# Attention fused with an RWKV channel mix on one core: a new written-out order of pieces, with four zeros matmuls fewer

## The chip, the cores and the metric

The kernel runs on 1 core of one Trainium2 chip (8 cores, of which one is used). The metric is the device time of one execution in microseconds. TensorE is called PE here, VectorE DVE, ScalarE ACT, GpSimd POOL and SyncE SP.

## The reference

For 8 batches, 8 heads, 576 rows and a head width of 64, a linear attention is followed by a channel mix of width 512 with a hidden width of 1024:

```python
kv = np.einsum('bhsd,bhse->bhde', k, v)
u = np.einsum('bhsd,bhde->bhse', q, kv)
rms = np.sqrt(np.mean(u * u, axis=-1, keepdims=True) + 1e-06)
x = (u / rms * g_norm)             # heads side by side: (B, S, 512)
x_prev = x shifted by one row
xk = mu_k * x + (1.0 - mu_k) * x_prev
xr = mu_r * x + (1.0 - mu_r) * x_prev
kk = np.maximum(xk @ w_k, 0.0)
out = sigmoid(xr @ w_r) * (kk * kk @ w_v)
```

All inputs and the output are fp32; the kernel multiplies in bf16.

## The kernel before

The work is cut into some 660 named pieces. Each piece issues a handful of instructions on one engine, and a string `ORDER` names them one after another. `Plan.emit` walks through that string and calls each piece; nothing is rearranged afterwards, so an engine runs its pieces in the order of the string, and an engine that waits holds up everything behind it in its own queue. A suffix `@A` or `@D` puts a piece on ACT or DVE where both can do it. `z:512` issues one matmul of zeros with 512 columns (line 437, into a PSUM buffer that the first stage-two product will overwrite).

A batch `b` goes through attention, with `z` (0 or 1) the half of the heads. For batch 0 the halves are separate pieces; for later batches one piece `.01` does both.

- `ldh.k`, `ldh.v`: SP loads the first half of k and v of batch 0 as fp32 (line 236, into memory that later holds `xk`); `cst.k0`, `cst.k1`, `cst.v0`, `cst.v1` cast them to bf16 (lines 128 on ACT, 130 on DVE).
- `ld.*`: POOL issues all other loads of q, k, v (lines 221, 226) and of the weights (line 252), which cast on the way. POOL's own queue waits for buffers and for a free slot of eight.
- `kv`: k transposed times v on PE (line 265). `kc` copies it, `ks` permutes it on PE (line 271), `kd` copies it again.
- `tq`: DVE transposes q (line 349). `u`: q times kv on PE (line 282).
- `uc`: u times g_norm into SBUF (lines 134, 136). `sq`: the squares, on ACT (line 370).
- `ss`, `rs`: sums of squares on PE (lines 395, 379) and reciprocal root on ACT (line 288). From batch 2 on `rs` is made once per head and `sp` spreads it over partitions with four DMAs of SP each (line 417).
- `mul` (line 392), `d` (line 300), `mk`/`mr` (lines 134, 136), `xk`/`xr` (line 313): the normed x, its difference to the row before, and the two blends.

Rows are then taken in nine groups `g` of 512: `k` (xk times w_k, lines 469 for g = 0, 493), `relu` (ACT, line 452), `ksq` (DVE, lines 480, 503), `r` (xr times w_r, line 515), `sig` (ACT, line 525), `v` (times w_v, line 535), `out` (the product, DVE, lines 548, 562), `st` (SP stores 128 rows, line 443). `tr9`, `cols` and `small` bring mu_k, mu_r and g_norm into columns: four small loads on SP, one fp32 matmul (line 211) and two DVE copies (lines 200, 201).

PSUM has four buffers `ps`, given out in turn. Two engines that read the same PSUM buffer wait for one another in the order of the string.

## Time and profile before

| | us |
|---|---|
| median of 3 timed runs | 201.87 (201.4 to 201.99) |
| the profiled execution, own time | 203.93 |
| its span from first to last instruction | 202.2 |
| PE busy | 190.9 |
| DVE busy | 134.3 |
| ACT busy | 125.0 |
| first matmul of zeros starts | 1.19 |
| last packet of `ldh.v` / `ldh.k` | 4.75 / 9.43 |
| first `kv` matmul starts | 9.97 |
| second `kv` starts | 15.14 |
| end of the last matmul | 198.2 |

The page gives busy time by engine; PE's is a model, as matmuls overlap, so the spacing of their starts tells more: 0.216 us between two matmuls of 512 columns at the full granted clock, and 0.427 us before 5.2 us. In the stretches (windows) each engine has its busy time and, in brackets, its number of instructions; then come the granted clock, the DMA share and GB/s. In the chain of waits each row is start, length, engine and line. In the timeline a row is start, length, engine, line, operation, what it writes and reads, how many, and in brackets how long the engine was idle before it and who ended that.

### The profile page before, as it was taken

The numbers are of one execution on the slowest core, as the hardware profiler recorded it, in microseconds if no ns is written. First come the engines' busy times: TensorE is split into PE (matmuls) and PEld (weight loads), VectorE is DVE, ScalarE is ACT, GpSimd is POOL, SyncE is SP. The second block draws the span as 40 slices with busy tenths as digits, with TensorE's granted clock in tenths as the row PEclk, the third lists the DMA queues.
The fourth block names the chain that finished last, engine by engine and source line by source line (L and its number), as shares of the span: only waits on it lengthen the run. The fifth ranks groups of instructions, "written<-read, shape, count | busy, mean of one in ns | idle before, by whom it ended". The sixth has DMA issues, their size and how long they took to land.

```text
span 202.2 us, 4282 instructions
## 1 busy us (share of the span) xinstructions
PE 190.9 (94%) x1769; PEld 93.8 (46%) x1769; DVE 134.3 (66%) x238; ACT 125.0 (62%) x163; POOL 23.3 (12%) x41
## 2 busy tenths in 40 slices
PE   7499897999999899999999999999999999999992
...
PEclk9999999999999999999999999999999999999999
...
GB/s 208 213 209 207 211 203 205 216 203 212 208 234 241 273 245 264 211 217 93 259 9 58 165 83 143 174 35 3 24 197 105 0 128 134 0 0 0 156 159 156
DMA packets 21015, 30.63 MB, mean 151 GB/s; under 512 B 1916, under 2 KB 14468, under 8 KB 20996
## 3 DMA queue, kind: packets, MB, share of 16 engines
...
q10 hardware_dynamic: 144, 0.13, 0.2%
...
## 4 chain that ended last, share of the span: by engine, by line
PE 76%; DMA 8%; DVE 7%; ACT 6%; SPq 1%; issue 1%; DVEq 0%
PE ps L535 28%; PE ps L493 26%; PE ps L515 14%; DMA xk<-in_k_dram 4%; DMA rs<-rsc 4%; ACT relu L452 2%; PE ps L282 2%; PE ps L265 2%; PE ps L437 1%; DVE xk L313 1%; DVE md L136 1%; DVE d L300 1%; ACT md L134 1%; DVE xT L392 1%; DVE uT L136 1%; ACT rs L288 1%
## 5 line engine op out<-in xcount | busy, mean ns | idle before, releaser
L535 PE MATMUL ps<-w_v,sqk 128*128 128x512 bf16 (+1 forms) x296 | 66.3, 373 | 0.9 <-ACT sq L370 0.9
L493 PE MATMUL ps<-xk,w_k 128*128 128x512 bf16 (+1 forms) x288 | 58.9, 356 | 1.0 <-DVE xk L313 1.0
L452 ACT ACTIVATE relu<-ps 128x1024 bf16<-128x1024 f32 x36 | 35.8, 1024 | 29.9 <-PE ps L493 28.9
L535 PEld LDWEIGHTS <-sqk 128*128 128x128 bf16 x296 | 28.3, 98 | 33.8 <-issue 2.7
L493 PEld LDWEIGHTS <-w_k 128*128 128x128 bf16 x288 | 27.3, 98 | 28.0 <-issue 1.9
L515 PE MATMUL ps<-w_r,xr 128*128 128x512 bf16 x144 | 34.4, 379 | 0.0
L548 DVE TENSOR_TENSOR out<-ps,sig 128x1024 f32<-128x1024 f32 x16 | 19.5, 1223 | 21.4 <-PE ps L535 9.4
L503 DVE TENSOR_TENSOR sqk<-relu 128x1024 bf16<-128x1024 bf16 x32 | 21.3, 686 | 12.4 <-ACT relu L452 12.4
L525 ACT ACTIVATE sig<-ps 128x1024 bf16<-128x1024 f32 x18 | 18.2, 1022 | 13.4 <-PE ps L515 13.2
L370 ACT ACTIVATE sq<-ps 128x576 bf16<-128x576 f32 x32 | 19.9, 653 | 4.8 <-PE ps L282 3.0
L515 PEld LDWEIGHTS <-xr 128*128 128x128 bf16 x144 | 13.8, 98 | 15.7 <-issue 0.2
L392 DVE TENSOR_TENSOR xT<-uT,rs 128x1152 bf16<-128x1152 bf16 (+1 forms) x18 | 12.3, 685 | 7.6 <-ACT rs L288 4.3
L136 DVE TENSOR_SCALAR md<-d,cols 128x576 bf16<-128x576 bf16 (+1 forms) x52 | 15.7, 352 | 0.4
L144 ACT ACT_TABLE_LOAD x12 | 15.4, 1283 | 0.9 <-PEq L588 0.7
L134 ACT ACTIVATE uT<-ps,cols 128x576 bf16<-128x576 f32 x19 | 13.6, 744 | 1.2 <-PE ps L282 1.1
L136 DVE TENSOR_SCALAR uT<-ps,cols 128x576 bf16<-128x576 f32 x13 | 10.5, 815 | 5.2 <-ACT sq L370 3.3
L134 ACT ACTIVATE md<-d,cols 128x576 bf16<-128x576 bf16 (+1 forms) x20 | 12.7, 699 | 1.6 <-DVE d L300 1.6
L437 PE MATMUL ps<-zero 128*128 128x512 bf16 x43 | 12.4, 435 | 1.2 <-DVE zero L164 1.2
L313 DVE TENSOR_TENSOR xk<-md,xT 128x1152 bf16<-128x1152 bf16 (+1 forms) x18 | 12.3, 688 | 1.8 <-ACT md L134 1.4
L313 DVE TENSOR_TENSOR xr<-md,xT 128x1152 bf16<-128x1152 bf16 (+1 forms) x18 | 12.0, 686 | 2.1 <-ACT md L134 2.0
L349 DVE STREAM_TRANSPOSE qT<-q 128x576 f32<-128x576 f32 (+1 forms) x18 | 13.2, 761 | 0.1
L300 DVE TENSOR_TENSOR d<-xT 128x1152 bf16<-128x1152 bf16 (+1 forms) x18 | 12.4, 692 | 0.4
...
## 6 DMA issues: line engine op xcount, KB each, us to landing
...
```

The lines of the kernel that those rows point to most:

```text
L134: nc.scalar.mul(out=dst, in_=src, mul=col)
L136: nc.vector.tensor_scalar(out=dst, in0=src, scalar1=col, scalar2=None, op0=ALU.mult)
L144: nc.scalar.preload_act_table_set(name)
L313: nc.vector.tensor_tensor(out=dst[:, 2 * z:2 * z + 2, r0:r0 + w], in0=md.t[:, :, cs], in1=xT[:, :, cur], op=ALU.add)
L370: sq_ = add("sq" + name, "A", lambda _, ps=ps, sq=sq, cs=cs, w=w: nc.scalar.activation(out=get(sq)[:, :, cs], in_=ps.t[:, :, 0:w], func=AF ...
L452: nc.scalar.activation(out=get(rt), in_=ps.t, func=AF.Relu)
L493: nc.tensor.matmul(get(ps)[:, fc % 2, a0:a1], w_k_sb[:, cc, 128 * fc:128 * fc + 128], xk[:, cc, x0:x0 + a1 - a0], start=(cc == 0), stop=(c ...
L503: nc.vector.tensor_mul(out=get(sqk)[:, 2 * f2:2 * f2 + 2, :], in0=rt.t, in1=rt.t)
L515: nc.tensor.matmul(get(ps)[:, ci % 2, :], xr[:, cc, n0:n0 + 128], w_r_sb[:, cc, :], start=(cc == 0), stop=(cc == NHP - 1))
L525: nc.scalar.activation(out=get(sg), in_=ps.t, func=AF.Sigmoid)
L535: nc.tensor.matmul(get(ps)[:, bank, cs], sqk.t[:, fc, 128 * ci:128 * ci + 128], w_v_sb[:, fc, cs], start=(fc == 0), stop=(fc == NFC - 1))
L548: dv = add(f"out{g}.{c2}", "D", lambda _, ps=ps, sg=sg, ot=ot: nc.vector.tensor_mul(out=get(ot), in0=ps.t, in1=sg.t), deps=ms + [sg_done], ...
```

## The change

`ORDER` is replaced by another one; no other line changes. The new string comes from a new search of the order and of the engines of all pieces, which was given later landings of the first loads, and in which the number of zeros matmuls is the least that a nominal and a late course ask for. It has 39 zeros matmuls instead of 43. All other pieces are the same. The beginning of the string, up to the two first weight products, as it was and as it is (the 16 zeros ahead of `kv0.0` and the loads ahead of them are the same):

```diff
- cst.v1@D cst.v0@A cst.k0@D cst.k1@D (z:512 x16) kv0.0 kc0.0@A z:512 z:512 ks0.0 tq0.0.0 tq0.0.1 tq0.1.0 small
-   z:512 z:512 tr9 cols kd0.0@A u0.0.1 uc0.01@A sq0.01 tq0.1.1 z:512 u0.0.0 sq0.00 (z:512 x7) kv0.1
-   ld.v3.01 ld.k3.01 ld.q3.01 uc0.00@D kc0.1@A ss0.01 ss0.00 rs0.01 ks0.1 mul0.01 kd0.1@A rs0.00 mul0.00
+ cst.v1@D cst.v0@A cst.k0@D cst.k1@A (z:512 x16) kv0.0 kc0.0@A z:512 z:512 ks0.0 tq0.0.0 tq0.0.1 tq0.1.0 small
+   tr9 cols kd0.0@A u0.0.1 uc0.01@A sq0.01 u0.0.0 uc0.00@D sq0.00 (z:512 x6) kv0.1
+   ld.k3.01 ld.v3.01 kc0.1@A ss0.01 tq0.1.1 ld.q3.01 ss0.00 rs0.01 mul0.01 ks0.1 kd0.1@A rs0.00 mul0.00
  (z:512 x3) u0.1.1 uc0.11@D sq0.11 u0.1.0 sq0.10 (z:512 x11) ss0.10 uc0.10@A d0.00 mk0.00@D xk0.00 k0.000
- k0.010 d0.01 mr0.01@D mk0.01@D xk0.01 ss0.11 rs0.10 mul0.10 d0.10 mr0.10@A k0.110
+ d0.01 mr0.01@D mk0.01@D xk0.01 ss0.11 rs0.10 mul0.10 d0.10 mr0.10@A k0.010 k0.110
```

Behind that, pieces change places all through the string, mostly by one to five positions. Those that change an engine or a queue's order, or that the prediction speaks of:

```diff
- relu0.11 u1.01.0 uc1.10@A ksq0.10 sq1.10 uc1.00@D u1.01.1
+ relu0.11 u1.01.0 uc1.00@D uc1.10@A ksq0.10 sq1.10 u1.01.1
- mul1.1 ss1.1 rs1.1 r0.0 r0.1 rs1.0 xr0.01 xr0.11 r0.2 mul1.0 d1.0 r0.3 d1.1
+ ss1.1 mul1.1 d1.1 rs1.1 r0.0 r0.1 rs1.0 xr0.01 xr0.11 r0.2 mul1.0 d1.0 r0.3
- kc2.01@A out0.1 k1.4 ... sp2.0 ... kv3.01 ld.k5.01 ld.q4.01 ld.v6.01 ld.v5.01 st0.1 st0.3 ksq1.1 st0.0
+ kc2.01@A out0.1 st0.3 k1.4 ... sp2.0 ... kv3.01 ld.k5.01 ld.q4.01 ld.v6.01 ld.v5.01 ld.q5.01 st0.1 ksq1.1 ... st0.0
- kv4.01 ld.k7.01 ld.q6.01 ld.v7.01 ld.q5.01 d2.1 uc3.00@A ss3 v1.2.1 ... k2.0 kd4.01@D ... k2.4 k2.1
+ ss3 d2.1 uc3.00@A kv4.01 ld.k7.01 ld.q6.01 ld.v7.01 v1.2.1 ... k2.0 k2.1 kd4.01@A ... k2.4
- kc6.01@D sp4.0 xr3.0 st2.2
+ kc6.01@A xr3.0 st2.2 ksq3.0 sp4.0
- uc6.10@D u6.01.1 xr4.0 uc6.00@A
+ uc6.10@D xr4.0 u6.01.1 uc6.00@D
- relu5.2 mr5.1@A xr5.1
+ mr5.1@D relu5.2 xr5.1
- mk6.0@D sq7.00 uc7.00@A r5.2 r5.3 ss7 mr6.1@D xk6.0 out5.0 rs7 k6.0 sp7.0 k6.1 xr6.1 st5.0
+ mk6.0@A sq7.00 uc7.00@A r5.2 r5.3 ss7 mr6.1@D xr6.1 xk6.0 out5.0 st5.0 rs7 sp7.0 k6.0 k6.1
```

More of the change, by code (lines that the diff above doesn't have):

```diff
@@ L15 @@
 ORDER = """
-ldh.v ldh.k ld.q0.0 ld.q0.1 ld.v0.1 ld.k0.1 ld.v1.0 seta zz setb setp ident perm ld.wk0 ld.k1.1 ld.wk1 ld.v1.1 ld.k1.0 ld.q1.01 ld.wv0 ld.wv1 ld.wr ld.k2.01 ld.v2.01 ld.q2.01 table cst.v1@D cst.v0@A cst.k0@D cst.k1@D z:512 z:512 z:512 z:512 z:512 z:512 z:512 z:512 z:512 z:512 z:512 z:512 z:512 z:512 z:512 z:512 kv0.0 kc0.0@A z:512 z:512 ks0.0 tq0.0.0 tq0.0.1 tq0.1.0 small z:512 z:512 tr9 cols kd0.0@A u0.0.1 uc0.01@A sq0.01 tq0.1.1 z:512 u0.0.0 sq0.00 z:512 z:512 z:512 z:512 z:512 z:512 z:512 kv0.1 ld.v3.01 ld.k3.01 ld.q3.01 uc0.00@D kc0.1@A ss0.01 ss0.00 rs0.01 ks0.1 mul0.01 kd0.1@A rs0.00 mul0.00 z:512 z:512 z:512 u0.1.1 uc0.11@D sq0.11 u0.1.0 sq0.10 z:512 z:512 z:512 z:512 z:512 z:512 z:512 z:512 z:512 z:512 z:512 ss0.10 uc0.10@A d0.00 mk0.00@D xk0.00 k0.000 k0.010 d0.01 mr0.01@D mk0.01@D xk0.01 ss0.11 rs0.10 mul0.10 d0.10 mr0.10@A k0.110 mk0.10@D xk0.10 k0.001 k0.011 rs0.11 mul0.11 relu0.00 d0.11 mk0.11@A xk0.11 ksq0.00 kv1.01 ld.k4.01 ld.v4.01 kc1.01@D mr0.00@D mr0.11@A relu0.01 k0.100 k0.101 relu0.10 tq1.01.1 tq1.01.0 ks1.01 kd1.01@A ksq0.01 k0.111 relu0.11 u1.01.0 uc1.10@A ksq0.10 sq1.10 uc1.00@D u1.01.1 sq1.11 ksq0.11 uc1.11@A sq1.00 v0.0.0 v0.1.0 xr0.00 xr0.10 ss1.2 sq1.01 rs1.2 ss1.3 rs1.3 v0.0.1 uc1.01@D ss1.0 v0.1.1 mul1.1 ss1.1 rs1.1 r0.0 r0.1 rs1.0 xr0.01 xr0.11 r0.2 mul1.0 d1.0 r0.3 d1.1 sig0.0 mk1.0@D xk1.0 sig0.1 out0.0 v0.2.0 v0.3.0 v0.3.1 v0.2.1 mk1.1@A xk1.1 mr1.0@A kv2.01 ld.k6.01 kc2.01@A out0.1 k1.4 ks2.01 kd2.01@A tq2.01.0 tq2.01.1 k1.5 relu1.2 u2.01.0 sq2.10 uc2.00@D sq2.00 uc2.10@D k1.2 k1.3 u2.01.1 sq2.11 uc2.01@D uc2.11@D k1.6 k1.7 mr1.1@D xr1.1 sq2.01 ss2 rs2 sp2.1 relu1.1 xr1.0 sp2.0 k1.0 k1.1 relu1.0 kv3.01 ld.k5.01 ld.q4.01 ld.v6.01 ld.v5.01 st0.1 st0.3 ksq1.1 st0.0 r1.0 r1.1 tq3.01.1 ksq1.0 r1.2 kc3.01@D relu1.3 ksq1.3 ks3.01 tq3.01.0 r1.3 kd3.01@D sig1.0 u3.01.1 uc3.01@D sig1.1 v1.3.0 v1.2.0 sq3.01 ksq1.2 sq3.11 u3.01.0 uc3.10@A uc3.11@D mul2.1 v1.3.1 v1.0.0 sq3.00 v1.0.1 sq3.10 kv4.01 ld.k7.01 ld.q6.01 ld.v7.01 ld.q5.01 d2.1 uc3.00@A ss3 v1.2.1 mul2.0 d2.0 mk2.0@D v1.1.0 v1.1.1 mk2.1@A xk2.1 kc4.01@A ks4.01 rs3 xk2.0 k2.0 kd4.01@D out1.0 out1.1 mr2.0@A xr2.0 k2.4 k2.1 mr2.1@D xr2.1 k2.6 relu2.0 k2.5 relu2.2 tq4.01.1 tq4.01.0 ld.q7.01 k2.2 ksq2.2 ksq2.0 k2.3 relu2.1 k2.7 ksq2.1 relu2.3 st0.2 r2.2 sp3.0 ksq2.3 u4.01.0 sq4.10 r2.3 sig2.1 mul3.0 v2.1.0 d3.0 v2.0.0 mk3.0@D sp3.1 mr3.0@D sq4.00 uc4.00@A mul3.1 xk3.0 v2.1.1 v2.2.0 st1.3 uc4.10@A v2.3.0 u4.01.1 sq4.11 v2.2.1 v2.0.1 d3.1 mk3.1@D v2.3.1 xk3.1 sq4.01 uc4.01@A r2.0 st1.2 uc4.11@A r2.1 mr3.1@A out2.1 k3.0 sig2.0 k3.1 out2.0 k3.2 kv5.01 relu3.0 kv6.01 xr3.1 kc5.01@D ss4 rs4 sp4.1 k3.3 ks5.01 relu3.1 kc6.01@D sp4.0 xr3.0 st2.2 ksq3.0 ksq3.1 k3.4 k3.5 r3.0 kd5.01@A relu3.2 tq6.01.0 ksq3.2 ks6.01 kd6.01@A r3.1 sig3.0 st1.0 tq6.01.1 tq5.01.0 st2.3 k3.6 k3.7 relu3.3 v3.3.0 tq5.01.1 u5.01.0 sq5.00 uc5.00@A uc5.10@A sq5.10 v3.2.0 r3.2 r3.3 sig3.1 mul4.1 u5.01.1 d4.1 sq5.01 uc5.11@A uc5.01@A ksq3.3 v3.3.1 v3.2.1 st1.1 mk4.1@D v3.0.0 xk4.1 mul4.0 d4.0 sq5.11 out3.1 v3.0.1 u6.01.0 mk4.0@D xk4.0 ss5 rs5 mr4.1@D sp5.1 mr4.0@D v3.1.0 v3.1.1 out3.0 sp5.0 sq6.00 sq6.10 k4.2 k4.3 relu4.1 k4.0 k4.1 uc6.10@D u6.01.1 xr4.0 uc6.00@A sq6.01 k4.4 k4.5 st3.2 ksq4.1 uc6.11@D uc6.01@D st3.3 sq6.11 kv7.01 kc7.01@D ss6 relu4.0 ksq4.0 relu4.2 rs6 k4.6 k4.7 relu4.3 sp6.0 xr4.1 r4.2 mul5.1 r4.3 d5.1 mk5.1@D v4.0.0 ksq4.3 ksq4.2 sig4.1 st2.1 v4.3.0 tq7.01.0 st2.0 xk5.1 v4.1.0 v4.1.1 r4.0 ks7.01 kd7.01@A mul5.0 d5.0 mr5.0@A mk5.0@D xk5.0 sp6.1 r4.1 sig4.0 tq7.01.1 mul6.0 v4.2.0 v4.2.1 v4.3.1 out4.1 st4.2 st4.3 v4.0.1 out4.0 xr5.0 k5.4 k5.5 st4.0 k5.2 relu5.2 mr5.1@A xr5.1 k5.3 relu5.1 d6.0 mr6.0@D ksq5.1 k5.0 u7.01.1 uc7.01@A uc7.11@A k5.1 k5.6 k5.7 st4.1 sq7.11 ksq5.2 relu5.0 ksq5.0 relu5.3 ksq5.3 r5.0 r5.1 v5.1.0 mul6.1 sq7.01 d6.1 mk6.1@D v5.1.1 sig5.0 xk6.1 u7.01.0 sq7.10 uc7.10@A v5.2.0 v5.0.0 v5.0.1 mk6.0@D sq7.00 uc7.00@A r5.2 r5.3 ss7 mr6.1@D xk6.0 out5.0 rs7 k6.0 sp7.0 k6.1 xr6.1 st5.0 k6.2 k6.3 xr6.0 relu6.0 k6.4 relu6.1 ksq6.0 mul7.0 k6.5 d7.0 relu6.2 mr7.0@D ksq6.2 st3.0 ksq6.1 sig5.1 sp7.1 mul7.1 d7.1 v5.3.0 v5.3.1 st5.1 xr7.0 mk7.0@D xk7.0 r6.0 r6.2 r6.3 sig6.1 r6.1 k6.6 k6.7 relu6.3 sig6.0 v6.3.0 v5.2.1 v6.2.0 st3.1 v6.1.0 ksq6.3 v6.1.1 out5.1 v6.3.1 v6.2.1 mk7.1@D xk7.1 k8.0 mr7.1@D xr7.1 k8.1 k8.2 v6.0.0 v6.0.1 out6.1 st6.2 out6.0 k8.3 relu8.1 relu8.0 k7.2 ksq8.1 st5.3 k7.4 k7.0 k7.5 relu7.2 ksq8.0 k7.3 relu7.1 ksq7.1 ksq7.2 k8.6 st5.2 st6.3 k7.6 k7.7 relu7.3 ksq7.3 k8.7 relu8.3 k7.1 relu7.0 v8.0.00 r7.0 st6.1 r7.1 sig7.0 k8.4 r7.2 r7.3 sig7.1 k8.5 relu8.2 ksq7.0 v7.3.0 v7.3.1 ksq8.3 v7.0.0 v7.2.0 v7.2.1 out7.1 st7.3 st7.2 r8.0 v7.0.1 r8.2 v7.1.0 v7.1.1 out7.0 st6.0 r8.1 sig8.0 r8.3 st7.1 st7.0 v8.2.00 sig8.1 ksq8.2 v8.0.10 out8.00 v8.1.00 v8.1.10 out8.10 st8.00 v8.2.10 out8.20 st8.10 v8.3.00 st8.20 v8.3.10 out8.30 st8.30 v8.3.01 v8.3.11 out8.31 st8.31
```

1 line of the change is left out of this document (added).

## The prediction

> **What bounds the kernel now.** I read the page's shares, then the stretches, the chain of waits, the timeline at the chain's stops.
>
> ```profile
> PE 190.9 (94%) x1769; PEld 93.8 (46%) x1769; DVE 134.3 (66%) x238; ACT 125.0 (62%) x163; POOL 23.3 (12%) x41
> PE   7499897999999899999999999999999999999992
> PEclk9999999999999999999999999999999999999999
> ```
> ```profile
> 10.00:25.00 15.00, 14.35 (x176) 8.40 (x177) 10.73 (x26) 8.66 (x16) 6.28 (x9) 1.00 1.15 209
> 25.00:68.00 43.00, 41.21 (x590) 21.21 (x588) 33.16 (x56) 38.32 (x55) 8.94 (x13) 1.00 1.18 218
> 68.00:198.00 130.00, 129.35 (x988) 62.14 (x988) 87.69 (x140) 76.06 (x92) 0.54 (x1) 1.00 0.45 119
> ```
>
> From 68 to 198 us TensorE lacks 0.65 us of being always busy, from 25 to 68 us 1.8 us. The work there is the same in both kernels. So time can come from the head (before 25 us), whose busy PE is partly zeros, and from the few stalls. The chain of waits through the head:
>
> ```profile
> 10.81 0.54 PE ps L437 x2
> 11.35 0.34 PE ps L271 x4
> 11.68 0.54 PE ps L437 x2
> 12.22 0.32 PE ps L211 x2
> 12.54 0.37 PE ps L282 x8
> 12.90 0.32 PE ps L437
> 13.23 0.37 PE ps L282 x8
> 13.60 1.62 PE ps L437 x7
> 15.21 0.70 PE ps L265 x36
> ...
> 24.60 1.05 PE ps L469 x8
> ```
>
> L437 is a matmul of zeros. Twelve of them lie on the chain: PE works through them in order while nothing that follows is waiting for anything else. They are filler that has become the bound. From the timeline:
>
> ```profile
> 4.77 0.67 ACT L128 CAST v<-xk 128x576 bf16<-128x576 f32 x1 [2.75 <-DMA xk<-in_v_dram]
> 9.45 0.83 DVE L130 CAST k<-xk 128x576 bf16<-128x576 f32 x2 [4.14 <-DMA xk<-in_k_dram]
> 11.72 0.36 ACT L128 CAST kv<-ps 64x256 bf16<-64x256 f32 x1 [0.51 <-PE ps L271]
> 13.26 0.74 POOL L252 DMA_DIRECT2D w_v<-in_moe_w_v_dram  x1 [0.87 <-DMA k<-in_k_dram]
> 24.22 0.74 POOL L226 DMA_DIRECT2D v<-in_v_dram  x1 [1.16 <-DMA k<-in_k_dram]
> 65.02 0.76 DVE L392 TENSOR_TENSOR xT<-uT,rs 128x1152 bf16<-128x1152 bf16 x1 [1.90 <-DMA rs<-rsc]
> 68.65 3.63 PE L493 MATMUL ps<-xk,w_k 128*128 128x512 bf16 x16 [0.98 <-DVE xk L313]
> ```
>
> POOL's slots tell when loads landed: `k0.1` (what `kv0.1` at 15.14 needs) before 13.26; its landing record says 12.97, `v0.1`'s 11.54. `kv0.1` had its data 2.2 us before it ran. The last two rows are the largest later stall.
>
> **The head, step by step** (times on the clock of the profile).
> 1. *Cast `k1` moves from DVE to ACT.* DVE cast both in 0.83 (to 10.28); ACT's cast of the same shape takes 0.67 (to 10.12). The second half of `kv0.0` waited until 10.34 for it; unhindered it follows at 10.28. Gain 0.06. DVE's three transposes (2.23) start at 9.84 instead of 10.20 and end at 12.07.
> 2. *Two zeros ahead of `tr9` go* (0.216 each by the spacing of starts, 0.43). `ks0.0` moves 11.28 to 11.22, `tr9` 12.15 to 11.56. `u0.0.1` could then start at 11.87, but needs ACT's copy `kd0.0`, which ends at 12.02: a new wait of 0.2. `u0.0.1` moves 12.47 to 12.09. Gain so far 0.38.
> 3. *One zero between `u0.0.1` and `u0.0.0` goes.* They stood 0.69 apart; two such groups without a zero stand 0.27 apart (17.52 and 17.79). `u0.0.0` now also needs a buffer that `cols` frees on DVE, at 12.27. It moves 13.16 to 12.36. Gain 0.80.
> 4. *Six zeros instead of seven ahead of `kv0.1`.* From `u0.0.0` to `kv0.1` were 1.98; less 0.216 is 1.77. `kv0.1` moves 15.14 to 14.13, still 1.16 after its load. **Gain 1.01.**
> 5. *`uc0.00` ahead of `sq0.00`, and ahead of the transpose `tq0.1.1`.* The two readers of one PSUM tile wait for each other: `uc0.00` (0.82) runs 12.85 to 13.67, `sq0.00` 13.69 to 14.28 (before: to 14.78). ACT is free when `kc0.1` wants it at 14.9. The transpose fills 13.6 to 14.4, where DVE would wait for `rs0.01` (16.33, now 15.3). Cost 0; without that cover 0.78.
> 6. From `kc0.1` to `k0.001` the chain (ACT copy, `rs`, DVE `mul`, `d`, `mk`, `xk`) has the same instructions on the same engines in the same order: 24.60 becomes 23.59. `ss0.11` (two matmuls, 0.25) moves ahead of `k0.010`; `rs0.11` waits for ACT's `mr0.10`, not for it. Cost 0.
> 7. *`uc1.00` on DVE ahead of `ksq0.10`.* `v0.0.0` needs that square, and starts at 32.74 when ACT's `sq1.10` ends. On DVE `u1.01.0` ends at 31.36, `uc1.00` takes 0.81, the square about 0.65: 32.77, so `v0.0.0` is released at about 32.84. Cost 0.1 (0 to 0.69, one square).
>
> Net at 33 us: 0.9 gained. (`d1.1`, 0.76, now goes ahead of `xr0.01` and `xr0.11` on DVE: they end at 37.6, `r0.2` wants them at 38.0.) Loads still in time there: `k1.0` landed 23.66 (used at 26.44, now 25.4), `w_r` 34.35 (37.17, now 36.3), `v2` 40.03 (44.17, now 43.2).
>
> **From 33 to 68 us.** SP issues `st0.3` before the spread `sp2` instead of behind it. It waits only for `out0.1`, over by 45.5, and SP has nothing else until 52. Its 256 KB at 218 GB/s push the queued loads back by 1.2: `q3` from 51.24 to 52.4, wanted at 53.9; `v4` from 56.93 to 58.1, wanted at 62.7. Cost 0.
> The stall at 68.65 is the open term. `k2.0` waits for `xk2.0`, that for `mul2.0`, that for the last part of `sp2.0`, issued at 57.82 and landed at 64.90. Its issue starts with `rs2` and so moves 0.9 forward. If it lands as long after its issue as before, the 0.9 is kept; if the load queue, which does not move, sets the landing, nothing is kept (k2.0 at 68.65 again); if it lands sooner, because one store less is behind it, up to 0.98 more comes. I take the first: seven of the eight landings lie 5.7 to 6.6 after their issue, which looks like latency behind a queue that is full in both kernels.
>
> **From 68 us.** Copies and scalings change engine (`kd4`, `kc6`, `mk6.0` to ACT; `uc6.00`, `mr5.1` to DVE), `st2.2` and `st5.0` go ahead of a spread on SP, pieces on PE change places. ACT has 54 of 130 us free, DVE 42. `sp4.0` behind `st2.2` lands up to 1.6 later (0.4 issue, 1.2 for 256 KB) than its last part's 100.8, and holds `mul4.0` (101.45) up to 0.9; behind that DVE idled 1.2 ahead of `out3.1` (104.22): covered. `mk6.0` on ACT takes 1.4 instead of DVE's 0.65, ends about 141.6 on the old clock, and `xk6.0` 142.4, 1.2 ahead of `k6.0` (143.59). `q5` on POOL goes ahead of `k7`, `q6`, `v7`, which come 2.8 later (one 576 KB load), to about 85 to 91; `kv7` is at 114, `tq6` after 94. I take 0, between +0.98 (one more wait like the largest) and -0.65 (all idle time there). The last four matmul groups, the last product and store are the same.
>
> **Sum.** -1.01 + 0.1 = -0.91. The profiled execution took 203.93 (span 202.2 and 1.73 around it); it would be 203.0. The median of the timed runs is 201.87, 2.06 below: **200.96, I say 201.0.** Where the profiled run lost 2 us the page does not say. Candidate: `ldh.k` took 8.19 to land, `ldh.v`, as large, 4.0; 15 of its 16 parts were there at 7.33.
>
> **Rivals.**
> *The gain is caught by transfers* (0.26; 201.3 to 201.87, likeliest 201.6). Place one: `sp2.0`, as above. Place two: if timed runs get `k` 2.1 earlier, `kv1.01` stood at 24.3 there and now wants 23.3, but `k1.0` lands at 23.66; 0.4 is lost, and more at `w_r` (34.35, wanted at 34.2) and `q3`. The planner assumed later first loads; with earlier ones its fillers matter less. For: loads fill the DMA until 93 us. Against: in the profile every load has over a microsecond to spare.
> *The clock falls* (0.10; 202.6). PE idles 2.99 before `kv0.0` while it waits for the cast. The first nine zeros started 0.427 apart, later ones 0.216, and the full clock came 4.0 after the first matmul. If the hole, or the thinner PE work behind it (four zeros less, 0.2 idle), brings half speed back, up to 4 us of head work double and PE's share of the chain there adds 1 to 2 us, eating the gain: -0.9 + 1.6. It decides once the granted clock shows less than 1.0 between 7 and 15 us. Against: it stayed at 1.0 through the same hole.
> The Trainium skill ("TensorE: Matmul & The Clock Gate", "HAM oscillation — how this bites in real kernels") names idle gaps over some 3.4 us as what halves the clock. By that rule the hole of 2.99 is short of it, and the trace agrees; a `k` that lands 0.5 later would cross it in both kernels.
> *An unforeseen wait in the new order* (0.06; 202.5): slower only if over 1.2 us, more than any stall after 33 us now.
> *It does nothing*: excluded for the zeros, which PE runs or does not run.
>
> **How the numbers follow.** The forecast (head gain kept, 200.4 to 201.25) has 0.58. About 0.3% (0.6 us) is what a measurement of this kernel tells from no change, so faster means under 201.26. Low end 200.3: 0.91 and two thirds of the stall at 68.65. High end 202.4: through the caught gain and into the slower cases, leaving out about 0.1 above.
>
> **What would show it.** Right: `kv0.1` near 14.1 (start of `kv0.0` as before), `k0.001` 1.0 earlier, first `L493` of stage two at about 67.7 with a wait near 1.0, PE idle after 68 us still under 1. Wrong: `kv1.01` waiting on a load, `mul2.0` still at 65.0, granted clock below 1.0 in the head, a new PE wait over 0.5 after 68 us, or `kv0.1` not moving.

## The result, and the profile after

The changed kernel took **200.31 us** (median of 4 executions, 200.21 to 200.39) and the kernel before 201.81 (4 executions, 201.40 to 201.99) on the same chip: a ratio of 0.9922, 95% interval 0.9906 to 0.9939. (The ratios here and below leave out executions that took over 1.5% more than the fastest of their kernel.) That is 1.5 us faster where 0.9 was forecast. The profiled execution took 200.31 too, with a span of 198.5 and 1.8 around it.

The page's shares and slices of the changed kernel, as for the kernel before:

```profile
PE 187.8 (95%) x1742; PEld 93.3 (47%) x1765; DVE 135.1 (68%) x236; ACT 126.4 (64%) x165; POOL 23.2 (12%) x41
PE   7899879999999999999999999999999999999992
PEclk9999999999999999999999999999999999999999
```

TensorE is still busy nearly everywhere, and the clock stood at 1.0 in this execution. In the place in which the chain of waits listed twelve zeros matmuls before, it has:

```profile
7.15 13.14 DMA w_k<-in_moe_w_k_dram
...
22.09 20.43 DMA q<-in_q_dram
```

From 7 to 42 us the work that ended last is now two loads, with an issue of POOL and 1 us of waiting for it between them. The timeline at the places that the prediction went by:

```profile
5.91 0.80 DVE L130 CAST k<-xk 128x576 bf16<-128x576 f32 x1 [0.97 <-DMA xk<-in_k_dram]
7.34 2.24 DVE L349 STREAM_TRANSPOSE qT<-q 64x576 f32<-64x576 f32 x3 [0.64 <-DMA q<-in_q_dram]
...
9.88 0.44 PE L282 MATMUL ps<-qT,kv 32*64 32x288 bf16 x8 [0.47 <-DVE cols L201]
10.25 1.47 PE L437 MATMUL ps<-zero 128*128 128x512 bf16 x6
11.65 0.76 PE L265 MATMUL ps<-v,k 64*64 64x64 bf16 x36
...
64.85 2.34 DVE L548 TENSOR_TENSOR out<-ps,sig 128x1024 f32<-128x1024 f32 x2
65.07 7.07 PE L493 MATMUL ps<-xk,w_k 128*128 128x512 bf16 x32 [0.30 <-DVE xk L313]
```

`k`'s first half was cast from 5.91 (9.45 in the profile of before, whose `ldh.k` landed 3.5 us later). `kv0.1` runs at 11.65, and its data `k0.1` landed at 11.56: the margin of 2.2 us is down to 0.1. What PE did wait for stands a little earlier: `u0.0.0` (9.88) waited 0.47 for `cols`, which DVE could only do behind three transposes of q, and those began when the first part of q had landed, at 7.32. The row with L548 x2 is the largest surprise: `out1.0` and `out1.1` run back to back, with no wait in front of either, and behind them PE's 32 matmuls of the next products are one unbroken row.

That profile of before had an unusually late `ldh.k`. A second profile of the kernel before (e1) is the fairer one to set beside the changed kernel: span 200.4, `kv0.0` at 7.57, `kv0.1` at 12.73, `k0.1` landed at 11.64. It has this in DVE's and PE's timeline:

```profile
65.81 1.21 DVE L548 TENSOR_TENSOR out<-ps,sig 128x1024 f32<-128x1024 f32 x1
69.35 1.22 DVE L548 TENSOR_TENSOR out<-ps,sig 128x1024 f32<-128x1024 f32 x1 [2.32 <-DMA out_dram<-out]
70.62 2.75 PE L493 MATMUL ps<-xk,w_k 128*128 128x512 bf16 x12 [0.56 <-DVE out L548]
```

DVE stands still for 2.32 us ahead of `out1.1`. There are three `out` buffers; `out1.1` needs the one of `out0.0`, and that is free only when `st0.0` has landed. SP issued `st0.0` at 58.60, behind `st0.1` and `st0.3`, and it landed at 69.33, 10.7 us later. PE needs the PSUM buffer that `out1.1` reads, and loses 0.56 at once. The chain of waits of that run goes straight through it:

```profile
58.60 10.72 DMA out_dram<-out
...
69.35 1.22 DVE out L548
```

In the changed kernel `st0.3` is gone from in front of it (issued at 42.48, landed at 48.98), `st0.0` landed at 64.12, and the wait is not there. `k2.0`, the first of these products, starts at 65.57 in e1 and at 65.07 in the changed kernel; of the 1.9 us between the two spans 1.4 thus lie behind it. So three theories were set against one another: **H**, the head's gain carries to the end; **S**, the gain is that of `st0.3`'s place; **R**, the new order of the pieces behind the head has a share. **L** is the rival of H by which loads limit the head. A fourth came up with the runs: **C**, the granted clock.

### The profile page after: what moved, and what is told of

Its sections match the earlier page's. It is cut to its first block, busy times and chain, and to the rows that moved or that the text cites. A ratio compares the mean times of both kernels' runs of the same rounds, so it can differ in the third digit from the quotient of the medians.

```text
span 198.5 us, 4240 instructions
## 1 busy us (share of the span) xinstructions
PE 187.8 (95%) x1742; PEld 93.3 (47%) x1765; DVE 135.1 (68%) x236; ACT 126.4 (64%) x165; POOL 23.2 (12%) x41
## 4 chain that ended last, share of the span: by engine, by line
PE 65%; DMA 20%; DVE 4%; POOL 3%; issue 2%; SPq 2%; ACT 1%; POOLq 0%; DVEq 0%
PE ps L493 25%; PE ps L535 24%; PE ps L515 12%; DMA q<-in_q_dram 10%; DMA w_k<-in_moe_w_k_dram 7%; DMA rs<-rsc 3%; SPq L417 2%; PE ps L282 2%; PE ps L265 1%; POOL v L226 1%; DVE xT L392 1%; DVE qT L349 1%; DVE xk L313 1%; ACT L144 1%; POOL q L221 1%
## 5 line engine op out<-in xcount | busy, mean ns | idle before, releaser
L535 PE MATMUL ps<-w_v,sqk 128*128 128x512 bf16 (+1 forms) x286 | 64.9, 373 | 1.8 <-ACT sq L370 0.8
L548 DVE TENSOR_TENSOR out<-ps,sig 128x1024 f32<-128x1024 f32 x16 | 19.4, 1222 | 19.0 <-PE ps L535 10.1
L136 DVE TENSOR_SCALAR md<-d,cols 128x576 bf16<-128x576 bf16 (+1 forms) x52 | 16.2, 358 | 0.4
L136 DVE TENSOR_SCALAR uT<-ps,cols 128x576 bf16<-128x576 f32 x14 | 11.3, 816 | 4.0 <-PE ps L282 2.1
L134 ACT ACTIVATE uT<-ps,cols 128x576 bf16<-128x576 f32 x18 | 12.9, 744 | 1.5 <-DVE cols L201 1.0
L437 PE MATMUL ps<-zero 128*128 128x512 bf16 x37 | 10.7, 442 | 1.5 <-DVE zero L164 1.2
```

The lines of the kernel that those rows point to most:

```text
L134: nc.scalar.mul(out=dst, in_=src, mul=col)
L136: nc.vector.tensor_scalar(out=dst, in0=src, scalar1=col, scalar2=None, op0=ALU.mult)
L535: nc.tensor.matmul(get(ps)[:, bank, cs], sqk.t[:, fc, 128 * ci:128 * ci + 128], w_v_sb[:, fc, cs], start=(fc == 0), stop=(fc == NFC - 1))
L548: dv = add(f"out{g}.{c2}", "D", lambda _, ps=ps, sg=sg, ot=ot: nc.vector.tensor_mul(out=get(ot), in0=ps.t, in1=sg.t), deps=ms + [sg_done], ...
```

## How the experiments are read

Every execution comes with its mean granted clock. Most show 0.995 to 1.0; some show 0.983 to 0.992 and are longer, kernel by kernel, by 1.0 to 2.5 us in the median. One stretch of 3.41 us at half clock makes 1 - 0.5 x 3.41 / 201 = 0.9915. Executions at 0.993 or below are counted as "fallen", and medians of the others ("clock up") are given beside the ratio. The medians with the clock up are the ones to compare, since the ratios hold another share of the fallen executions for each kernel.

| | median, all | ratio to before on that chip (95%) | clock up: median (n) | fallen |
|---|---|---|---|---|
| before, chip of e1 to e4 | 202.30 | | 202.03 (26) | 9 |
| e1 before again | 202.18 | 1.0029 (0.9991 to 1.0067) | 202.13 (7) | 1 |
| e2 zeros only | 201.65 | 0.9975 (0.9928 to 1.0022) | 201.18 (7) | 5 |
| e3 head only | 202.84 | 1.0009 (0.9963 to 1.0055) | 200.74 (5) | 7 |
| e4 rest only | 200.66 | 0.9951 (0.9917 to 0.9986) | 200.62 (10) | 2 |
| before, chip of e5 to e8 | 201.97 | | 201.28 (29) | 6 |
| e5 store only | 200.64 | 1.0001 (0.9962 to 1.0041) | 200.60 (10) | 2 |
| e6 changed, store back | 202.27 | 0.9995 (0.9947 to 1.0044) | 200.86 (6) | 6 |
| e7 four `out` buffers | 201.35 | 0.9989 (0.9947 to 1.0030) | 201.04 (9) | 3 |
| e8 changed, zeros back | 200.81 | 0.9948 (0.9907 to 0.9989) | 200.75 (10) | 2 |
| before, chip of e9 to e12 | 202.63 | | 202.09 (19) | 8 |
| e9 changed again | 200.71 | 0.9917 (0.9886 to 0.9948) | 200.65 (10) | 2 |
| e10 changed + filler | 200.69 | 0.9908 (0.9872 to 0.9943) | 200.69 (6) | 0 |
| e11 e8 + filler | 201.05 | 0.9940 (0.9910 to 0.9971) | 201.05 (10) | 0 |
| e12 e5 + filler | 200.88 | 0.9947 (0.9914 to 0.9980) | 200.88 (12) | 0 |
| before, chip of e13 to e16 | 202.62 | | 202.11 (15) | 8 |
| e13 before + filler | 201.99 | 0.9955 (0.9925 to 0.9985) | 201.99 (12) | 0 |
| e14 head + filler | 201.71 | 0.9948 (0.9908 to 0.9988) | 201.67 (10) | 2 |
| e15 store + filler | 200.88 | 0.9899 (0.9860 to 0.9939) | 200.88 (6) | 0 |
| e16 head + store + filler | 200.46 | 0.9880 (0.9836 to 0.9925) | 200.47 (6) | 0 |
| before, chip of e17, e18 | 202.05 | | 201.99 (11) | 3 |
| e17 changed + filler | 200.52 | 0.9930 (0.9894 to 0.9966) | 200.37 (7) | 2 |
| e18 head + store + filler | 200.22 | 0.9888 (0.9840 to 0.9937) | 200.21 (5) | 1 |

## First experiments: one part alone

**e1**, the kernel before, nothing edited.

> The kernel before, unchanged, for a second profile: the one shown has ldh.k landing at 9.43 us, the changed kernel's profile 5.89. Both theories: time 201.8. Theory H (the head's own gain carries to the end, and the 0.6 us above the forecast is a shorter stall at k2.0): with k early, kv0.1 stands at about 12.05, 0.4 behind the changed kernel's 11.65. Theory L (the landing of the loads limits the head, and what is gained lies between 25 and 68 us): the same 12.05, but k2.0 is about 1.5 later than the changed kernel's 65.07, that is about 66.6, so that 1.1 of the gain is made behind kv0.1.

Measured: 202.18; the profile is the one shown above. Both theories missed in the head, where `kv0.1` stood at 12.73 and not at 12.05, and L missed at `k2.0`: 0.5 behind the changed kernel and not 1.5. It gave the fair comparison, and the wait of 2.32 us.

**e2**, the four zeros only.

```diff
- small z:512 z:512 tr9 ... tq0.1.1 z:512 u0.0.0 sq0.00 (z:512 x7) kv0.1
+ small tr9 ... tq0.1.1 u0.0.0 sq0.00 (z:512 x6) kv0.1
```

> The kernel before with the same four zeros matmuls taken out at the same places and nothing else changed. Theory H: most of the gain, 0.9 to 1.0 us (200.8 to 200.9). Theory L: kv0.1 can start only 0.4 earlier (k0.1 lands at 11.56), and what follows does not carry even that in full: a gain of 0.2 to 0.5 us (201.3 to 201.6).

Measured: 201.65 in all, 201.18 with the clock up, 5 of 12 fallen; that is 0.85 below before and between H and L. The profiled execution was one in which the clock fell twice; its rows are shown under "The clock".

**e3**, the new order up to `ksq0.00`, the old one behind it.

```diff
- ORDER = (old, to ksq0.00) (old, from there)
+ ORDER = (new, to ksq0.00) (old, from there)
```

> The new order up to ksq0.00 (the whole head, with its 39 zeros), the old order from there on. Theory H: 0.9 to 1.5 us faster than before (200.3 to 200.9), about the changed kernel. Theory L: 0.2 to 0.5 us faster (201.3 to 201.6).

**e4**, the other half: old head with its 43 zeros, new order behind it.

```diff
- ORDER = (old, to ksq0.00) (old, from there)
+ ORDER = (old, to ksq0.00) (new, from there)
```

> The old order up to ksq0.00 with its 43 zeros, the new order from there on. Theory H: no gain of its own, 0 to 0.3 us (201.5 to 201.8), as the forecast had the rest at 0. Theory L: 0.9 to 1.3 us faster (200.5 to 200.9), with a wait ahead of k2.0 about 0.5 shorter than in the kernel before.

Measured: e3 scattered from 200.19 to 203.29 with 7 of 12 fallen; with the clock up 200.74, which is H's forecast, from 5 executions. Its `out1.1` waited 0.97. e4, which keeps every zeros matmul, came to 200.66, L's forecast, `out1.1` without a wait and a span of 198.6, all but the changed kernel's 198.5. So the part that was forecast to cost or bring nothing brings nearly the whole gain by itself, and H alone is refuted. But with the clock up the head by itself stands as low, and these two runs do not divide the gain.

**e5**, the kernel before with one word moved.

```diff
- out0.1 k1.4 ... st0.1 st0.3 ksq1.1 st0.0
+ out0.1 st0.3 k1.4 ... st0.1 ksq1.1 st0.0
```

> The kernel before with one piece moved: the store st0.3 stands right behind out0.1, ahead of the spread sp2, instead of between st0.1 and st0.0; nothing else changed. Theory S (the gain is a store's: out1.1 on DVE needs the buffer that st0.0 empties; with one store less ahead of it st0.0 lands sooner, and DVE, and then PE in stage two, stop waiting): out1.1 waits less than 0.5 for a store (2.32 us in the last profile of the kernel before), time 0.7 to 1.1 us below before, as the new order without its head gave. Rival R (the gain is the new order of the pieces k2 and v2 on PE and of the scalings on DVE, which needs fewer PSUM buffers at a time): no change, within 0.3 us of before.

Measured: 200.64, span 198.7, no wait at `out1.1`. The ratio by itself says no difference; the medians with the clock up, 200.60 against 201.28, say 0.7. Left unclear here, it was settled by e13 against e15.

**e6**, the opposite: the changed kernel with that word put back.

```diff
- out0.1 st0.3 k1.4 ... st0.1 ksq1.1 r1.0
+ out0.1 k1.4 ... st0.1 st0.3 ksq1.1 r1.0
```

> The changed kernel with st0.3 put back between st0.1 and st0.0, nothing else undone. Theory S: out1.1 waits 1 to 2.5 us for a store again, and 0.7 to 1.1 us of the gain are lost (about 201.0 to 201.4 where the changed kernel takes 200.3). Rival R: still the changed kernel's time, since the order of k2 and v2 stays.

Measured: `out1.1` waits again, 2.56 us for `st0.0`, and PE loses 0.35 behind it. From `k2.0` to the last instruction this run took 134.4 and e1 134.8; e4 took 133.3 and e5 133.5. The timed median is 202.27, but half of its executions are fallen. With the clock up it is 200.86, below the 201.0 to 201.4 that S had: 0.1 behind e8 on the same chip and 0.2 behind e9, the changed kernel itself on another.

**e7**, the kernel before with a fourth `out` buffer, which takes the wait away from the other side.

```diff
- "out": (3, (128, 2, C), FP32),
+ "out": (4, (128, 2, C), FP32),
```

> The kernel before in its old order, with four output buffers instead of three, so that out1.1 takes a buffer that no store has to empty first. Theory S: the wait of out1.1 is gone altogether though no store moved; 0.5 to 1.1 us below before. Rival R: no change. A third reading (the early store helps the spread sp2 to land sooner, not the buffer): no change here, but a gain in the kernel with the moved store.

Measured: no wait at `out1.1`, and from `k2.0` (66.48) to the end 133.5. Its head was late in the profiled execution (PE idle 1.01 ahead of `kv0.0`), so the span is 200.0. That it is the buffer that `out1.1` waits for is shown; the timed gain, 0.2 with the clock up, misses the 0.5 to 1.1 of S, and a difference of means of -0.29 with an interval from -1.05 to 0.63 takes in none and most of it.

**e8**, the changed kernel with the four zeros back.

```diff
- small tr9 ... u0.0.1 uc0.01@A sq0.01 u0.0.0 uc0.00@D sq0.00 (z:512 x6) kv0.1
+ small z:512 z:512 tr9 ... u0.0.1 uc0.01@A sq0.01 z:512 u0.0.0 uc0.00@D sq0.00 (z:512 x7) kv0.1
```

> The changed kernel with the four zeros matmuls put back where they stood, nothing else undone. If the head carries a gain to the end (theory H): 0.9 to 1.0 us slower than the changed kernel. If the loads limit it (theory L): 0 to 0.4 us slower, so 200.3 to 200.8 where the changed kernel takes 200.3; kv0.1 0.4 later than k0.1's landing allows.

Measured: 200.81, every execution with the clock at 0.995 or more below 200.92. What this kernel keeps is the store's place; the price of the zeros is too small to read here and was measured by e10 against e11.

## The clock

The scatter of these runs had to be explained before the parts could be sized. The stretches of e2 (same columns as above; clock, DMA share and GB/s last) are cut where its record of the clock changes, and one stretch ahead of each:

```profile
7.78:11.19 3.41, 2.50 (x41) 1.27 (x35) 3.21 (x6) 1.49 (x4) 1.80 (x4) 1.00 1.15 198
11.19:14.61 3.42, 3.42 (x44) 1.78 (x43) 0.82 (x1) 1.42 (x3) 1.81 (x3) 0.50 1.18 213
...
28.26:31.67 3.41, 1.89 (x39) 0.94 (x38) 3.41 (x7) 3.40 (x7) 0.54 (x1) 1.00 1.20 195
31.67:35.09 3.42, 3.42 (x10) 1.45 (x10) 1.57 (x4) 1.95 (x5) 0.74 (x1) 0.50 1.24 212
```

In these records the clock changes at whole stretches of 3.41 us. The one before a fall had PE busy for 2.50 and 1.89 of 3.41. The second place is the same in both kernels: PE waits 0.59 for DVE's transpose ahead of `u1.01.0` and 0.86 for ACT's square ahead of `v0.0.0`. In e6 the clock fell behind the same two waits, at 29.79. Where the stretches begin differs from run to run (the clock rises between 3.99 and 7.19 us), so at times both waits fall into one stretch (1.45 us or more idle), mostly they are divided. In the profiles without the filler below, the clock fell behind two of the three stretches that held both waits whole, and behind none of the others there (up to 1.28 idle). The third, in e9, shows that it is an edge and not a sharp rule:

```profile
27.25:30.67 3.42, 1.90 (x37) 0.92 (x37) 3.36 (x6) 3.41 (x7) 0.52 (x2) 1.00 1.21 195
30.67:34.08 3.41, 3.41 (x20) 1.76 (x18) 2.02 (x4) 2.78 (x5) 0.84 (x2) 1.00 1.24 209
```

Nor does the sum of idle time decide by itself. The first profile of the kernel before has this stretch in its hole ahead of `kv0.0`, with PE less busy than in any of those above, and the clock stayed at 1.00 in the next one:

```profile
5.17:8.59 3.42, 1.81 (x9) 0.59 (x6) 0.14 (x1) 0.27 (x1) 2.74 (x6) 1.00 1.08 214
```

The Trainium skill ("TensorE: Matmul & The Clock Gate", "What's actually happening" and "HAM oscillation — how this bites in real kernels") has a free-running window of 3413 ns, which these stretches agree with. It warns of idle gaps over some 3.4 us; here no single gap ahead of a fall was longer than 0.86, and the measurement decides.

To test it, the second of the two waits was filled: six matmuls of zeros into columns of `u1.01.1`'s PSUM buffer that nothing reads.

```diff
  def u_tiles(...):
      ...
+     for x in range(6 if (b, i) == (1, 1) else 0):
+         nc.tensor.matmul(pss[zs[-1]][:, x % 2, HS:512], zero[:, 0:128], zero[:, 0:512 - HS], start=True, stop=True)
```

**e9**, the changed kernel again, **e10** with the filler, **e11** with filler and the four zeros back, **e12** the kernel before with filler and `st0.3` moved:

> The changed kernel, unchanged, beside the kernels with filler, to see how its executions spread. Theory C (clock): the granted clock is set for stretches of 3.41 us, and a stretch in which PE idles 1.4 us or more is followed by one at half clock; the two waits of PE at 27.0 (0.59) and 28.6 (0.83) fall into one stretch in some executions and not in others, and the thinner head gives a second such place. Then some 4 to 6 of 12 executions show a mean granted clock near 0.991 and take 202.5 to 203.2, the others 200.2 to 200.9. Rival N (the clock falls for reasons outside the kernel): as rare as in the kernel before, 1 to 3 of 12. Theory S (st0.3's move shortens the executions whose clock stays up): those without the fall lie within 200.2 to 200.9.

> The changed kernel with six matmuls of zeros of 224 columns at the end of u1.01.1, into columns of its PSUM buffer that nothing reads; they fill most of PE's wait of 0.83 at 28.6. Theory C: no stretch of 3.41 us around 30 us holds over 1.0 of idle time any more, so only the head (7 to 12 us) can still bring the clock down: 0 to 3 of 12 executions with a mean granted clock near 0.991, median 200.3 to 200.7. Rival N: the share of such executions is as in the changed kernel itself, and the median too. Cost of the filler in the others: 0 (PE waits there anyway), at most 0.2.

> The changed kernel with its four zeros back at their old places and with the filler at the end of u1.01.1. Theory C: neither the head nor the place near 30 us leaves a stretch with 1.4 of idle time, so 0 or 1 of 12 executions shows a clock near 0.991; all take 200.3 to 201.0, median 200.7, highest below 201.5. Rival N: 2 or more of 12 at 202.5 to 203.

> The kernel before with two edits only: st0.3 right behind out0.1, and the filler at the end of u1.01.1. Theories S and C: st0.0 is back in time for out1.1 and the clock stays up, so 200.4 to 201.0 in all but 0 or 1 of 12 executions, as good as the changed kernel or better. Rival R (the new order of the pieces behind the head is worth something of its own): 0.3 or more behind the changed kernel with filler.

PE's timeline in e10 (line numbers are two higher behind the edit):

```profile
29.55 0.75 PE L286 MATMUL ps<-zero 128*128 128x224 bf16 x6
30.47 0.81 PE L537 MATMUL ps<-w_v,sqk 128*128 128x512 bf16 x2 [0.18 <-ACT sq L372]
```

The wait of 0.86 is 0.18, and `v0.0.0` stands 1.87 behind `u1.01.0` here as in e9. Fallen: e9 2 of 12, e10 to e12 none of 28. e9's 2 are what N had, fewer than the 4 to 6 of C; taken alone they tell nothing. Counted over all runs: with the old number of zeros in the head, 44 of 190 executions without the filler and 0 of 40 with it; with the thinner head, 20 of 52 without and 5 of 39 with it. The falls left are put down to the head. In the profile of e14, which has filler and thin head, the clock fell there:

```profile
7.78:11.19 3.41, 2.38 (x30) 1.22 (x27) 2.66 (x6) 1.40 (x4) 1.74 (x4) 1.00 1.16 200
11.19:14.61 3.42, 3.42 (x44) 1.70 (x42) 1.37 (x2) 1.45 (x4) 1.86 (x3) 0.50 1.17 211
```

So C is right that PE's waits near 30 us bring the clock down, and N, by which falls come from outside the kernel, is refuted there. For the head there is one profile with filler, and the count of 5 of 39 against 0 of 40. C's limit of 1.4 us is wrong: falls came behind 0.91 (e2) and 1.03 us of idle time (e14), and none behind 1.52 (e9) and 1.61 (before). What makes the difference is open. e11 missed its forecast of 200.7 by 0.35: with the clock up in both, the four zeros cost 0.36 (e10 against e11); two of its executions, 201.77 and 202.80, also lie above the 201.5 that C had as its highest, with the clock up. e9 against e10 shows no cost of the filler (0.04). e12 came to 200.88, as forecast, but 0.19 behind e10 and not level with it. In the first comparison, of 4 executions each, no clock of the changed kernel was below 0.998, and the kernel before, at 201.40 to 201.99, was where it is elsewhere with the clock up (202.0), so the 1.5 us are not the clock's.

## The two parts crossed

With the filler in all four, on one chip: neither part, the new head, the store, both.

> The kernel before with only the filler at the end of u1.01.1 (order of before, store of before). Theory C: none of its executions has a mean clock near 0.991, and its median is that of the executions of before whose clock stays up, 201.3 to 202.1; the executions at 203.3 and more are gone. Rival N: some are still there.

> New order up to ksq0.00 (four zeros fewer, k1's cast on ACT), the rest and the stores as before, with the filler. Theory H (the head is worth 0.4 to 0.9 of its own): 0.4 to 0.9 below e13. Theory S (st0.0's landing sets out1.1, so an earlier head is lost there): within 0.3 of e13. out1.1 then waits 1 to 2.5 us for st0.0 in the trace.

> Old head, st0.3 right behind out0.1, filler. Theory S: 0.8 to 1.3 below e13, out1.1 without a wait. Theory H: within 0.4 of e13. Earlier 200.88.

> New head and st0.3 right behind out0.1, the rest as before, with the filler. If the two add: as far below e15 as e14 is below e13. If both only remove the same wait, or the loads take the head's gain: within 0.2 of e15. Theory R (the new order behind the head has a share of its own): 0.3 or more above the changed kernel with filler, 200.69.

DVE's timeline in e13 and the issues of SP's queue there (`x4` are `st0.1`, `st0.3`, `st0.0`, `st0.2`):

```profile
69.02 1.23 DVE L550 TENSOR_TENSOR out<-ps,sig 128x1024 f32<-128x1024 f32 x1 [1.88 <-DMA out_dram<-out]
...
57.73 1.84 SPq L445 DMA_DIRECT2D out_dram<-out  x4
```

and in e15:

```profile
65.51 2.35 DVE L550 TENSOR_TENSOR out<-ps,sig 128x1024 f32<-128x1024 f32 x2
...
42.91 0.38 SPq L445 DMA_DIRECT2D out_dram<-out  x1
...
57.13 1.51 SPq L445 DMA_DIRECT2D out_dram<-out  x3
```

One store less stands in front of `st0.0`: it landed at 69.00 in e13 and at 64.53 in e15. Medians with the clock up, and differences of means with 95% bootstrap intervals:

| | store as before | `st0.3` behind `out0.1` | difference |
|---|---|---|---|
| old head | 201.99 | 200.88 | -1.00 (-1.33 to -0.65) |
| new head | 201.67 | 200.47 | -1.01 (-1.52 to -0.49) |
| difference | -0.39 (-0.96 to 0.16) | -0.40 (-0.65 to -0.16) | both: -1.40 (-1.78 to -1.00) |

Here they add: the store is worth 1.0 and the head 0.4, together 1.4, close to the 1.5 of the whole change. The whole is firm, the division less so: the runs without the filler divide it otherwise. By means with the clock up and in front of the old store, the four zeros alone brought 0.83 in e2 (0.38 to 1.29) and the whole head 1.07 in e3 (0.59 to 1.56), and putting the store back cost 0.21 in e6 against e8 (-0.16 to 0.66). These are few executions, picked by their clock, and `out1.1`'s wait was shorter in the profiles of e2 and e3 (1.23 and 0.97) than in e14's. How much the head is worth in front of the old store, 0.4 or about 1, is open. In e14's profile the earlier head ran into the store, though its clock had fallen: `out1.1` waited 2.29 and PE lost 0.56 behind it. e14's place 0.3 below e13 is between what H and S expected, and its interval takes in none and all of H.

**e17 and e18** put the changed kernel and "head + store" side by side, both with the filler:

> The changed kernel with the filler, beside e18 on one chip. Theory S with a small share of the head: 200.4 to 200.8, as e18. Theory R (the rest of the new order is worth 0.3 or more): that much below e18.

> The kernel before with the new head, with st0.3 behind out0.1, and with the filler: within 0.2 of e17 if the rest of the new order is worth nothing; 0.3 or more above it if it is. A version ahead of both kernels if it stays at 200.5 or below.

Measured: 200.37 and 200.21 with the clock up, difference of means 0.23 (-0.11 to 0.54). Everything else in the new order, some sixty moves, brings nothing that these runs can show; R, which had e17 0.3 or more below e18, is refuted as a gain. e18 also is the best version found: 0.9888 of the kernel before (0.9840 to 0.9937), at least level with the changed kernel on the same chip. The kernel before needs for it the new head, one word moved, and six matmuls.

## Why the prediction was right and wrong

**Steps 1 to 4, the head's 1.01: the mechanism was right, the size holds only where loads do not bind.** The steps put 4.16 between `kv0.0` and `kv0.1` (14.13 - 9.97), where it was 5.17. e18's timeline shows them when `k0.1` had landed in time, at 11.60:

```profile
7.91 0.76 PE L265 MATMUL ps<-v,k 64*64 64x64 bf16 x36
...
12.02 0.76 PE L265 MATMUL ps<-v,k 64*64 64x64 bf16 x36
```

4.11, as worked out. But the steps were worked out on an execution whose `ldh.k` was late, and there every other load was in time. In the changed kernel `kv0.1` stands 4.77 behind `kv0.0`, and the row that says why is `u0.0.0`'s wait of 0.47 shown above: step 3 had `cols` done 0.09 ahead of it, with DVE's transposes following `k`'s cast at once. With `k` early they wait for q, which landed at 7.32, and `u0.0.0` stands 3.00 behind `kv0.0` instead of 2.39. From there to `kv0.1` it is 1.77, exactly step 4. So it is the landing of q, and not that of `k0.1` which L had named, that cuts the head's gain first; the zeros that went had hidden DVE's part of it. The profiles of the new head whose clock was up there have 4.11 to 4.95 between `kv0.0` and `kv0.1`, those with the four zeros and an early `k` 5.08 to 5.46.

The margins behind that are thin too: even with the four zeros `kv0.1` stands only 0.15 (e5) to 1.22 (e11) behind `k0.1` when `k` is early, and not 2.2. In the changed kernel `kv1.01` runs at 23.26 with `k1.0` landed at 23.22, and `r0.0` at 34.11 with `w_r` landed at 34.06; by the distance to the matmuls ahead of them, against e1, that cost 0.1 and 0.2. These two are the rival "the gain is caught by transfers", place two, at the places and nearly at the times that it named; q in the head it did not name. Its mechanism was right; as a forecast of the time it failed, since another gain more than made up for it. Little of the head is left at `k2.0`: with `k` early and no fall ahead it starts at 65.21 to 65.70 with the four zeros (8 profiles, mean 65.48) and at 64.96 to 65.95 without them (7, mean 65.34). What the head keeps in time, 0.4 by the crossed runs, is open to the doubt named there, and in which later wait it is kept is not settled by the traces.

**Step 5** held: `mul0.01` stands 1.96 behind `kv0.1` in the changed kernel and in e1, so no wait was added, and `k0.001` comes 9.67 behind `kv0.1`, 9.55 in e1. **Step 7**'s 0.1 is not seen: PE waits 0.83 ahead of `v0.0.0`, 0.86 before.

**"From 33 to 68 us ... Cost 0" is the step that failed.** It looked at whom `st0.3`'s early transfer pushes back (the loads; `q3` landed at 51.71 instead of 51.24, forecast 52.4, and nobody waited) and, at the stall of `k2.0`, at what a store less would do for the spread. It did not ask who waits for the stores left behind. The row was in the trace of before:

```profile
71.16 1.23 DVE L548 TENSOR_TENSOR out<-ps,sig 128x1024 f32<-128x1024 f32 x1 [1.10 <-DMA out_dram<-out]
```

`out1.1` waited 1.10 for `st0.0` there. With late `k` the stall of 0.98 at `k2.0` covered it, and PE lost nothing. With an early `k` that cover is gone. Of the six profiles with the store at its old place and `k` early, four (e1, e6, e13, e14) have a wait of 1.9 to 2.6, and PE pays for it: 134.4 to 134.8 from `k2.0` to the last instruction, against 133.3 to 133.8 in all others. The two others waited 0.97 (e3) and 1.23 (e2), and PE paid nothing. Mis-sized by 1.0, it is the missing part of the sum: the crossed runs give 0.4 for the head where the forecast had 0.9, and 1.0 for the store where it had 0. Two terms were off in opposite ways, so the sum looks better than its parts.

**The stall at `k2.0`** was put at about 0.98, unchanged; it is 0.30 in the changed kernel and 0.21 in e1, which has the old order. Spread `sp2.0`'s last part landed 6.2 us after its issue (before 7.1). The long stall belonged to the late profile: with `k` early and no fall it is 0.60 or less in all others. The low end of the range, 200.3, was the head's 0.91 and two thirds of this stall; that the time came out there is luck, since neither is what was gained.

**"From 68 us ... 0" held.** The trace shows no PE wait over 0.2 there that was not there before, and e17 against e18 finds no effect of the moves.

**"The clock falls"** had the chance of a side case, 0.10, and was put at the hole ahead of `kv0.0` or "the thinner PE work behind it". The second is what happens: e2 and e14 fell at 11.19, after a stretch from 7.78. A fall, there or near 30 us, costs 1.0 to 2.5 us in the median of a kernel's executions, against the 1.6 that the rival had, but only in part of them (20 of 52 with the thin head, 44 of 190 with the old one, without filler). It decided the median in e3 and e6, where half or more were fallen, and not in the changed kernel (0 of 4, then 2 of 12). The sign to look for, a granted clock below 1.0 between 7 and 15 us, was the right one. That both kernels have a second such place near 30 us was missed.

**The base.** "Where the profiled run lost 2 us the page does not say" and the candidate `ldh.k` were right: every other profile has `k` landed by 5.9 to 7.2, save e7 with 8.06, and a span of 201.0 or less, save e2 with its two falls. The forecast moved its sums from that run to the median by subtracting 2.06. But the late `k` had changed which waits were covered, so a constant could not be carried over.
